# Preparing more chunks two ahead, and another order of the loads, in an attention and experts kernel

## The chip, the cores and the metric

The kernel runs on one core of one Trainium2 chip. The metric is the device time of one execution, in microseconds (us).

## The reference, cut to what matters

Three stages follow each other. A gated linear attention walks 768 tokens for each of 4 x 8 heads of width 48; its output, as 3072 tokens of 384 features, goes through a wide layer with a squared relu, and then through a soft mixture of 8 experts with 4 slots each.

```python
f = 1.0 / (1.0 + np.exp(-f_logit))
for t in range(S):                      # 768 steps, every head at once
    state = f[:, :, t, :, None] * state + np.einsum('bhd,bhe->bhde', k[:, :, t], v[:, :, t])
    y[:, :, t] = np.einsum('bhd,bhde->bhe', q[:, :, t], state)
x = y.transpose(0, 2, 1, 3).reshape(3072, 384)
h = np.maximum(x @ w_in, 0.0)           # 384 -> 2048
x = h * h @ w_out                       # 2048 -> 384
logits = x @ phi                        # 32 slots; softmax over tokens, and over slots
...                                     # slot inputs through the experts (384 -> 1024 -> 384), combined back
```

## The kernel before, in words

**Chunks.** The attention is worked in 24 chunks of 128 tokens (6 for each of the 4 sequences). For each chunk a load `fkq` (672 KB: gate logits, keys and queries, L136) and a load `v` (192 KB, L138) are issued by `chunk_load`. `fkq` lands in one of three places, chunk i in place i % 3, each with one buffer; `v` has three buffers. `prep(i)` turns them into running products of the gates (ACT L156, L158 or DVE L160, then four scans on DVE, L162), their inverses (ACT L169, L170), scaled keys (DVE L171) and scaled queries (DVE L177, L178, L179). The place of `fkq` is free again when the last of these, L179, has read it. `chunk(i)` is the rest: transposed keys (PE L193, ACT L195), scores (PE L205, DVE L208), states (PE L220, DVE L226 or L228), values (PE L243 and L250, ACT L254, DVE L259). Its six result DMAs (L265, L268) write the chunk into the token block `x`, on the SP queue, as every DMA of the kernel does.

**Blocks.** Four chunks make a block of 512 tokens, and there are 6 blocks. The wide layer goes over 16 slices of the hidden width, a step (b, ff) for each block and slice: layer 1 (three passes per product, L118 to L120, through `mm3`), relu and square on ACT (L369, L371, L372), the low part on DVE (L374), and layer 2 into three PSUM banks. The first four steps of block 0 run instead on whole fp32 weights (`layer1_whole`, L353, and L384). `TURNS` sets the order: block 0 with slices 0 to 3, block 1 with slices 0 to 8, then the remaining slices of both, then blocks 2 to 5 one by one.

**Weights.** Each slice's weights come as int64 patterns of a float64 (`w_load`, 768 KB, L305) and are split by ACT (L315, L319) and DVE (L320, L321, and L331 or L333), then into a high and a low part (L113, L114).

**What sets the order.** `stream()` writes out prep and chunk in pieces, five to a chunk (`STEPS`); `upto` draws as many pieces as a step's target wants. Before the first step of the wide layer, `FIRST` = 23 pieces are drawn, that is chunks 0 to 3 and three pieces of chunk 4. While i + 2 < `AHEAD` the chunk i carries prep(i + 2) with it, and from there on prep(i + 1). The text of the program is not its order on the engines: a scheduler takes the instructions by priority, which is the order in which they are written, and by when it reckons that their operands are ready; each engine, SP's queue too, then runs its own list strictly in that order and waits where a semaphore is not there yet. What `high_priority()` encloses is put ahead of what was written before.

**The loads.** Chunks 0 to 2 are loaded at the start, then two weight slices. Chunks 3 and 4 are loaded when chunks 0 and 1 are written to their end, each followed by one weight slice; from chunk 5 on chunk i + 2 is loaded in the second piece of chunk i. Further weight slices come at the head of a step (`while len(raw) < ...`), so that four are ahead of the one to be split.

Of the kernel before, what the change touches and what calls it, by code (L numbers as in the profile page):

```python
# [7 lines left out]
F32 = mybir.dt.float32  # L8
# [17 lines left out]
DM = H * D  # L26
NCH = B * S // C
# [8 lines left out]
SLOTS = 3  # L36
RAW = 5
WAHEAD = 4
AHEAD = 5
FIRST = 23  # L40
WARM = (3, 1, 3, 3)
OT = 1
# [15 lines left out]
class K:  # L58
# [70 lines left out]
    def chunk_load(self, i):  # L129
        nc, ap = self.nc, self.ap  # L130
        fkq = self.slot(i % SLOTS)[:DD].rearrange("d (x p t) -> d x p t", x=3, p=NP)
        if i == 0:
            nc.sync.dma_start(out=fkq[:, 0], in_=self.A["fkq"][i][:, 0])
            nc.sync.dma_start(out=fkq[:, 1:], in_=self.A["fkq"][i][:, 1:])
        else:
            nc.sync.dma_start(out=fkq, in_=self.A["fkq"][i])  # L136
        v = ap.tile([128, DM], F32, tag="v", name="v", bufs=3)
        nc.sync.dma_start(out=v, in_=self.A["v"][i])  # L138
        return fkq[:, 0], fkq[:, 1], fkq[:, 2], v

# [534 lines left out]
    def fast(self):  # L675
        with ExitStack() as main:
            self.fresh()
            self.wp = self.pool(main, "wp", bufs=NFF)
            fst = main.enter_context(ExitStack())
            self.fp = self.pool(fst, "fp")  # L680
            wst = fst.enter_context(ExitStack())
            self.wr = self.pool(wst, "wr")
            self.gp = self.pool(main, "gp", side="right")
            ast = main.enter_context(ExitStack())
            self.ap = self.pool(ast, "ap", side="right")
            self.attention_state(self.ap)
            self.loaded[0] = self.chunk_load(0)
            self.consts2()
            for i in (1, 2):
                self.loaded[i] = self.chunk_load(i)  # L690
            raw = {ff: self.w_load(ff) for ff in range(2)}
            pst = fst.enter_context(ExitStack())
            self.fast_blocks(main, pst, ast, wst, raw)
            self.tail()

    def fast_blocks(self, main, pst, ast, wst, raw):

        def stream():
            for i in range(2):
                yield from self.prep(i)  # L700
            for i in range(NCH):
                ahead = 2 if i + 2 < AHEAD else 1
                ch = self.chunk(i)
                pr = self.prep(i + ahead) if i + ahead < NCH and i + ahead not in self.U else iter(())
                for j, n in enumerate((1, 1, 0, 0, 2) if ahead == 2 else (1, 1, 1, 0, 2)):
                    next(ch)
                    for _ in range(n):
                        next(pr, None)
                    new = i + 3 if i < 2 else i + 2
                    if j == (4 if i < 2 else 1) and i != 2 and new < NCH:  # L710
                        self.loaded[new] = self.chunk_load(new)
                        if new < 5:
                            more_w()
                    yield

        def more_w():
            if len(raw) < NFF:
                raw[len(raw)] = self.w_load(len(raw))

        st = stream()  # L720
        for _ in range(8):
            next(st)
        done = 0
        end = NCH * STEPS

# [29 lines left out]
        def begin1(b, ff):  # L755
            if b == 0 and ff < WHOLE:
                return self.layer1_whole(b, ff)
            split(b)
            part(ff)
            return self.layer1(b, ff)  # L760
# [7 lines left out]
        self.w_split(0, raw[0], True)  # L768
        wn = 1
        posts = iter(())  # L770
        pend = begin1(0, 0)
        wait = 0
        for n, (b, ff) in enumerate(steps):
            if n == 3:
# [211 lines left out]
```

## Time and profile before

| | |
|---|---|
| runs | 601.58, 605.31, 607.11 us; median 605.31 |
| profiled execution | 606.27 us, its span 604.5 us |
| PE | 574.9 us busy, 5587 matmuls |
| DVE | 328.7 us busy |
| ACT | 314.8 us busy |
| DMA | 69.59 MB, mean 115 GB/s |

The span is what the profiler saw of one execution, and 1.8 us of its time lie around it. PE's busy time is modelled from pipelined matmuls: an engine that reads full may still run at half its clock, so a stretch is read with the granted clock beside it, and with how long equal groups of matmuls took. The profile's slices show DVE and ACT full up to about a quarter of the span and half idle behind it, while PE is full nearly all the way from there.

### The profile page before, as it was taken

What the parts mean: (1) busy time and instruction counts of PE and PEld (TensorE: products, weight loads), DVE (VectorE), ACT (ScalarE), POOL (GpSimd) and SP (SyncE); (2) the same over time, 40 slices, a digit from 0 to 9 for tenths busy, and PEclk for the clock granted to TensorE, in tenths of its full rate; (3) what the DMA queues carried; (4) which work ended last, traced back from release to release, by engine and by line L of the source; (5) the groups of instructions that cost most, each with busy time, mean ns of one, the idle gap of its engine ahead of it and who ended that gap; (6) DMA issues with size and microseconds to landing.
All of it is one profiled execution on the core that took longest, in us unless ns stands there. A gap on an engine that the chain in (4) does not pass through costs nothing.

```text
span 604.5 us, 13326 instructions
## 1 busy us (share of the span) xinstructions
PE 574.9 (95%) x5587; PEld 442.4 (73%) x5587; DVE 328.7 (54%) x688; ACT 314.8 (52%) x577; POOL 4.0 (1%) x10
## 2 busy tenths in 40 slices
PE   4899899999999999999999999999999999998993
PEld 3784467788787878778877777887788887886372
DVE  6978989999825547454464552543332322213322
ACT  5647759996635546354455354544334544442122
POOL 0000000000000000000000000000000100000000
PEclk9999979999999999999999999999999999999898
DMA  9557558421321202202211210220000745554757
GB/s 290 181 154 236 160 190 287 151 67 47 105 60 40 73 2 73 59 16 73 73 46 28 74 63 18 79 79 3 15 14 12 263 135 177 168 199 157 262 205 272
DMA packets 28324, 69.59 MB, mean 115 GB/s; under 512 B 4464, under 2 KB 17008, under 8 KB 28256
## 3 DMA queue, kind: packets, MB, share of 16 engines
q1 hardware_dynamic: 28256, 68.65, 35.8%
q8 instruction: 46, 0.75, 0.5%
q14 instruction: 22, 0.18, 0.1%
HBM read 59.20 MB, written 4.72 MB: 106 GB/s over the span
## 4 chain that ended last, share of the span: by engine, by line
PE 77%; DVE 7%; DMA 6%; ACT 6%; issue 2%; SPq 1%; ACTq 0%; DVEq 0%
PE o L118 10%; PE ph L118 9%; PE o L120 9%; PE ph L120 9%; PE ph L119 9%; PE o L119 9%; DMA g<-fkq 4%; PE psm L243 3%; DMA raw<-w 2%; DVE ip L162 2%; PE hp L591 2%; PE psm L220 2%; PE psm L205 2%; PE so L615 2%; PE o L384 1%
## 5 line engine op out<-in xcount | busy, mean ns | idle before, releaser
L374 DVE TENSOR_TENSOR gl<-r,gh 128x512 fp32r<-128x512 f32 x92 | 63.5, 690 | 119.2 <-ACT r L372 118.6
L369 ACT ACTIVATE r<-ph 128x512 f32<-128x512 f32 x92 | 54.7, 595 | 119.9 <-PE ph L120 114.9
L118 PE MATMUL o<-gh,w 128*128 128x512 f32 x276 | 112.8, 409 | 0.0
L118 PE MATMUL ph<-x,w 128*128 128x512 f32 x276 | 111.5, 404 | 0.0
L119 PE MATMUL o<-gh,w 128*128 128x512 f32 x276 | 108.0, 391 | 0.0
L120 PE MATMUL o<-gl,w 128*128 128x512 f32 x276 | 106.3, 395 | 1.8 <-DVE gl L374 1.7
L120 PE MATMUL ph<-x,w 128*128 128x512 f32 x276 | 107.8, 391 | 0.0
L119 PE MATMUL ph<-x,w 128*128 128x512 f32 x276 | 107.6, 390 | 0.0
L120 PEld LDWEIGHTS o<-gl,w 128*128 128x128 f32 x276 | 51.6, 188 | 15.7 <-DVE gl L374 4.8
L118 PEld LDWEIGHTS ph<-x,w 128*128 128x128 f32 x276 | 51.8, 188 | 14.7 <-issue 4.1
L118 PEld LDWEIGHTS o<-gh,w 128*128 128x128 f32 x276 | 51.7, 187 | 12.6 <-ACT gh L371 0.5
L120 PEld LDWEIGHTS ph<-x,w 128*128 128x128 f32 x276 | 51.8, 188 | 11.5
L371 ACT ACTIVATE gh<-r 128x512 fp32r<-128x512 f32 x92 | 58.3, 634 | 2.0
L119 PEld LDWEIGHTS ph<-x,w 128*128 128x128 f32 x276 | 51.9, 188 | 9.7
L372 ACT ACTIVATE r<-r 128x512 f32<-128x512 f32 x92 | 58.0, 630 | 1.8
L119 PEld LDWEIGHTS o<-gh,w 128*128 128x128 f32 x276 | 51.9, 188 | 9.4
L156 ACT ACTIVATE g<-g 112x512 f32<-112x512 f32 (+1 forms) x25 | 15.1, 609 | 41.8 <-DMA g<-fkq 41.8
L243 PEld LDWEIGHTS psm<-q,S 48*48 48x48 f32 (+1 forms) x704 | 27.2, 147 | 9.7 <-issue 4.6
L243 PE MATMUL psm<-q,S 48*48 48x64 f32 (+1 forms) x704 | 31.5, 244 | 2.5 <-DVE S L226 1.3
L162 DVE TENSOR_TENSOR_SCAN ip<-g,ip,big 112x128 f32<-112x128 f32 x80 | 33.4, 467 | 0.4 <-ACT g L158 0.2
L220 PEld LDWEIGHTS psm<-v,n 64*48 64x48 f32 (+1 forms) x704 | 21.3, 146 | 10.8 <-issue 5.3
L169 ACT ACTIVATE g<-ip 112x512 f32<-112x512 f32 (+1 forms) x25 | 15.3, 611 | 26.2 <-DVE ip L162 26.1
(143 smaller groups left out, 683.0 us busy)
## 6 DMA issues: line engine op xcount, KB each, us to landing
m<-m SPq DMA_DIRECT2D x26, 768.0 KB, 4.4
g<-fkq SPq DMA_DIRECT2D x23, 672.0 KB, 5.2
raw<-w SPq DMA_DIRECT2D x16, 768.0 KB, 7.1
v<-v SPq DMA_DIRECT2D x24, 192.0 KB, 3.6
g<-m SPq DMA_DIRECT2D x6, 768.0 KB, 4.5
out_dram<-ob SPq DMA_DIRECT2D x18, 256.0 KB, 3.3
x<-y SPq DMA_DIRECT2D x48, 72.0 KB, 2.8
x<-y SPq DMA_DIRECT2D x48, 16.0 KB, 1.8
```

Source lines behind the costliest of these rows:

```text
L118: mm(out=out, lhsT=sh, rhs=mh, start=start, stop=False)
L119: mm(out=out, lhsT=sl, rhs=mh, start=False, stop=False)
L120: mm(out=out, lhsT=sh, rhs=ml, start=False, stop=stop)
L156: nc.scalar.activation(f[:, s], f[:, s], AF.Exp, scale=-1.0)
L162: nc.vector.tensor_tensor_scan(ip[:, p], f[:, p], big, 1.0 if first else self.ip[:, p, C - 1 : C], ALU.mult, ALU.min)
L169: nc.scalar.activation(f[:, s], ip[:, s], AF.Ln)
L220: nc.tensor.matmul(out=pu[c][m, p], lhsT=U["n"][r, p, m], rhs=U["v"][r, hd * D : hd * D + D], start=True, stop=True)
L243: nc.tensor.matmul(out=pz[h * HR : h * HR + m, p, r], lhsT=U["S"][c][d, p * D : p * D + m], rhs=U["q"][d, p, r], start=True, stop=True)
L369: nc.scalar.activation(r, o, AF.Relu)
L371: nc.scalar.activation(gh, r, AF.Square)
L372: nc.scalar.activation(r, r, AF.Square)
L374: nc.vector.tensor_tensor(gl, r, gh.bitcast(F32), ALU.subtract)
```

## The change

`AHEAD` goes from 5 to 9, so that chunks 0 to 6, and not only 0 to 2, carry the preparation of the chunk two behind them; chunk 7 then carries none. The buffer of `v` gets a fourth place. The load of chunk 3 is issued right after the first two preparations are written, and the load of chunk i + 4 in the first piece of chunk i (in the fourth piece from chunk 8 on). The first two weight slices move behind the load of chunk 3, and within the stream a weight slice is asked for in a chunk's last piece, after its results, if fewer than four are ahead. The first step of the wide layer is written under `high_priority()`.

```diff
-AHEAD = 5
+AHEAD = 9
...
-        v = ap.tile([128, DM], F32, tag="v", name="v", bufs=3)
+        v = ap.tile([128, DM], F32, tag="v", name="v", bufs=4)
...
-            raw = {ff: self.w_load(ff) for ff in range(2)}
+            raw = {}
...
-                    new = i + 3 if i < 2 else i + 2
-                    if j == (4 if i < 2 else 1) and i != 2 and new < NCH:
+
+                    new = i + SLOTS + 1
+                    if j == (0 if i + 1 < AHEAD else 3) and new < NCH:
                         self.loaded[new] = self.chunk_load(new)
-                        if new < 5:
-                            more_w()
+                    if j == 4 and len(raw) < wn + WAHEAD:
+                        more_w()
                     yield
...
         st = stream()
+        wn = 0
         for _ in range(8):
             next(st)
+        self.loaded[SLOTS] = self.chunk_load(SLOTS)
+        for _ in range(2):
+            more_w()
...
-        pend = begin1(0, 0)
+        with self.tc.high_priority():
+            pend = begin1(0, 0)
```

## Rows read from the trace of the kernel before

**Rows 1.** Stretches: start:end, length; busy us (instructions) per engine; granted clock; DMA.
```profile
0.00:45.50 45.50, 33.65 (x644) 30.03 (x644) 35.01 (x82) 24.70 (x45) 1.10 (x8) 1.00 0.69 207
45.50:87.00 41.50, 38.21 (x435) 21.61 (x433) 36.41 (x72) 28.67 (x52) 0.00 (x0) 0.92 0.62 185
87.00:150.00 63.00, 62.82 (x485) 49.53 (x484) 62.32 (x104) 54.02 (x96) 0.00 (x0) 1.00 0.45 151
150.00:190.00 40.00, 38.42 (x282) 30.10 (x280) 21.18 (x45) 21.91 (x40) 0.00 (x0) 1.00 0.27 71
190.00:540.00 350.00, 349.36 (x3114) 277.88 (x3115) 154.43 (x331) 170.45 (x315) 2.85 (x2) 1.00 0.24 74
```

**Rows 2.** PE's timeline: start, length, line, form, count, idle before it.
```profile
43.03 1.48 PE L243 MATMUL psm<-q,S 48*64 48x64 f32 x23
45.55 4.13 PE L353 MATMUL ph<-x,wn 128*128 128x512 f32 x6
57.06 0.85 PE L243 MATMUL psm<-q,S 48*64 48x64 f32 x22 [0.19 <-DVE S L228]
78.57 1.48 PE L243 MATMUL psm<-q,S 48*64 48x64 f32 x23
```

**Rows 3.** PE's waits over the span: total us, times, longest.
```profile
PE psm L220 <- ACT n L195: 2.1, 1, 2.1
PE ph L353 <- DVE wn L331: 0.9, 1, 0.9
```

**Rows 4.** The chain of waits from 64 to 76 us: start, length, what.
```profile
64.78 7.78 DMA raw<-w
72.59 0.26 ACT raw L315
...
74.56 0.43 ACT n L195
75.04 0.75 PE psm L220 x14
```

**Rows 5.** Stretches of 3 us around the wait, and 30 to 45 us.
```profile
75.00:78.00 3.00, 2.96 (x24) 1.37 (x26) 1.97 (x5) 1.75 (x3) 0.00 (x0) 0.58 1.04 302
78.00:81.00 3.00, 3.00 (x80) 2.94 (x77) 2.14 (x4) 0.66 (x2) 0.00 (x0) 0.50 0.68 257
81.00:84.00 3.00, 3.00 (x9) 1.44 (x7) 2.51 (x5) 2.35 (x5) 0.00 (x0) 0.78 0.13 29
30.00:45.00 15.00, 14.22 (x308) 12.89 (x307) 11.13 (x24) 7.10 (x13) 0.00 (x0) 1.00 0.58 156
```

**Rows 6.** SP's timeline: start, length, line, what is loaded, count.
```profile
5.44 0.81 SPq L305 DMA_DIRECT2D raw<-w  x2
8.90 0.33 SPq L136 DMA_DIRECT2D g<-fkq  x1
...
36.57 0.58 SPq L136 DMA_DIRECT2D g<-fkq  x1
...
63.69 0.58 SPq L136 DMA_DIRECT2D g<-fkq  x1
```

**Rows 7.** DVE's timeline, pieces of one preparation.
```profile
45.95 1.61 DVE L162 TENSOR_TENSOR_SCAN ip<-g,ip,big 112x128 f32<-112x128 f32 x4
47.86 0.69 DVE L171 TENSOR_TENSOR k<-g,ip 112x512 f32<-112x512 f32 x1
```

**Rows 8.** ACT's timeline, with the idle time before a row in brackets.
```profile
18.56 0.91 ACT L315 ACTIVATE raw<-raw 128x768 int32<-128x768 uint32 x1
37.86 0.93 ACT L315 ACTIVATE raw<-raw 128x768 int32<-128x768 uint32 x1 [2.35 <-DMA raw<-w]
42.68 0.63 ACT L156 ACTIVATE g<-g 112x512 f32<-112x512 f32 x1 [1.78 <-DMA g<-fkq]
```

**Rows 9.** The weight loads, L305: issue to landing.
```profile
DMA to landing us min/median/max: 4.4/7.1/13.5
```

**Rows 10.** SP's waits over the span: total us, times, longest.
```profile
SPq L136 <- DVE q L179: 161.6, 13, 20.2
```

## The prediction

> **What bounds the kernel now.** First the table of stretches [rows 1]: from 87 to 150 us PE is busy 62.82 of 63 us, from 190 to 540 us 349.36 of 350, both at the full clock. There no wait is left to take away; the change neither adds nor removes a matmul, so whatever it gains must come from before 87 us, from the 1.6 us that PE idles between 150 and 190, or from nowhere. The first 87 us are the stretch to read closely, and they have two halves. Up to 45.5 us only attention runs (chunks 0 to 4), DVE is busy 35.0 us and PE 33.7. From 45.5 to 87 us chunks 5 to 7 run between the four whole-weight steps, with PE at 38.2 of 41.5 and a granted clock of 0.92.
>
> The second view is PE's timeline, for how long equal work takes [rows 2]: 23 matmuls of L243 take 1.48 us at 43 us and again at 78.6, while 22 of them take 0.85 at 57. At 78 to 81 us the granted clock is 0.50, the 1.2 GHz level [rows 5]. So the first 45 us run at that level too, though the clock column reads 1.00 there; the first six L353 at 45.55 still straddle the change. In this half PE is slow, but a chunk there is paced by the ring of ACT, PE and DVE around it, not by PE alone.
>
> The third view is the chain of waits behind the low clock [rows 4]. A weight slice (the seventh) was issued at 64.78, right behind a chunk's load at 63.69 [rows 6], and landed 7.78 us later. ACT stood in front of it at L315, and behind L315 in ACT's list stood the copy L195 that chunk 7's states wait for; PE waited 2.1 us [rows 3], and then ran at 0.58, 0.50 and 0.78 of its clock through three stretches [rows 5].
>
> **The change, part by part.**
>
> *Chunk loads earlier.* SP issued chunk 5's load at 36.57 [rows 6], behind result DMAs, and ACT then waited 1.78 us for it and began that preparation at 42.68 [rows 8]. With the load written in chunk 1's first piece it goes ahead of the results that held it. The same holds for chunks 4 and 6 to 8, one load each. The number of loads stays 24, so SP and the DMA engines carry no more; only the place changes. Past that the loads are as late as their place allows already: 13 of them wait on SP for L179, 161.6 us in all [rows 10]. There I take nothing, and for the 1.6 us of PE idle between 150 and 190 us [rows 1] also nothing, with bounds of 1.6 us to either side.
>
> *The stall at 72 us.* Chunk 8's load is no longer in front of the seventh weight slice, as it is asked for four chunks ahead. The fastest weight load took 4.4 us, this one 7.8 [rows 4, 9]; 3.4 us less is more than ACT's wait, so the 2.1 us on PE should go, and with them the low clock: 0.42, 0.50 and 0.22 of 3 us are 3.4 us of full-clock time [rows 5]. Term: -5.5 us; bounds 0 (another wait takes its place) and -5.5. I take the whole, as the profile names both parts in one chain.
>
> *Preparations moved forward.* One preparation costs DVE 1.61 us of scans and 0.69 for keys [rows 7] ahead of the same chunk's state and values, and three more of about that 0.69 behind them, 4.4 us with the keys. In 30 to 45 us DVE idled 15 - 11.13 = 3.9 us [rows 5], which is the room for the fifth chunk's. What does not fit there delays chunk 3, and so block 0 and the first L353 at 45.55 [rows 2]: at worst 1.61 + 0.69 = 2.3 us. Against it, those 4.4 us leave the second half, where DVE is at 36.4 of 41.5 and L353 once waited 0.9 us for a split weight [rows 3]. Net between +2.3 and -0.9; I take +0.7, the middle.
>
> *The first two weight slices behind chunk 3's load.* They were issued at 5.44 and would now go after 8.90 [rows 6], since SP waits there for chunk 0's place. ACT took the second at 18.56 without a wait [rows 8]. Issued near 10 us and at the median 7.1 us [rows 9], it lands near 17. So 0, with an upper bound: at the longest landing seen, 13.5 us, it is there at 23.5, and ACT would stand some 5 us. The fourth `v` place lets chunk 3's `v` go without waiting, and what is queued behind it are these same two loads.
>
> The skill has a rule against this part. By the Trainium skill (DMA: Bandwidth & Descriptors, Queues, rings and completion order) each DMA engine consumes one queue's descriptors in ring order, so a load that is put in front delays all that follow, however urgent. By it alone the weights could not overtake, and the sum would be that of the slower rival below; that the chunk load at 63.69 stood in front of the weights that landed 7.78 us later agrees with it.
>
> *Weights behind results, high priority.* The third and fourth slices keep their places; later ones come up to a step sooner. The first L353 already begins right behind chunk 4's values, when block 0's last results have landed, so the priority can only move ACT's relu and square ahead of a preparation: 0, between -0.6 and +0.6, one ACT operation of a preparation [rows 8].
>
> **Sum.** 606.27 - 5.5 + 0.7 = 601.5 us, against the profiled execution, which was 0.96 us above the median of 605.31. So 0.6% below the median. A difference under 1%, some 6 us, I count as no change, about what a measurement of this kernel can tell.
>
> **Rivals.**
>
> *A. Everything in the second half goes.* If DVE has prepared ahead and no ACT wait is left, PE's idle 3.3 us there (41.5 - 38.21) and the missing 0.08 of the clock over 41.5 us, another 3.3 [rows 1], go: 606.27 - 6.6 = 599.7, and with DVE's earlier idle time used for up to 3.9 us more [rows 5], 595.8. For it: DVE has the room. Against: work is in engine order and some wait always comes last. 596.
>
> *B. The wait is replaced.* The scheduler orders ACT's list by reckoned landings. Another load, still 4.4 to 13.5 us long [rows 9], stands in front of another copy; ACT waited 2.35 us for a weight slice at 37.86 as well [rows 8], which the change leaves where it is. Then the low clock comes back too: 605 to 608, 606.
>
> *C. Slower: the weights arrive late at the start.* Place: ACT's L315 at 18.56, in front of chunk 2's work. It decides if the second slice lands later than that; each us beyond is a us for all of chunks 2 and 3, to which the 2.3 us of DVE work may come, while the wait at 72 moves along and stays. Price up to 5 + 2.3: 608 to 613.5, near 611. For it: two more DMAs in front in the busiest stretch of the loads. Against: the median landing leaves 1.5 us of room.
>
> *D. It does little because the scheduler had done it already.* The 13 waits for L179 [rows 10] say that for later chunks it had; for chunk 5, issued at 36.57 behind results [rows 6], it had not. I put this into B.
>
> **How the numbers follow.** My forecast, 597.5 to 605, has 0.44; A (594 to 597.5) 0.18; B 0.20; C 0.18. One third of the forecast's stretch lies below 599.3, so faster by over 1% has 0.18 + 0.15 = 0.33; slower, above 611.4, is half of C with a little of B's tail, 0.11; the rest, 0.56, is within 1%. The range 595 to 609 leaves out about a third of A and two thirds of C, 0.18 in all. The forecast's own range is 597.5 to 605.
>
> The clock part can be weighed once more. By the Trainium skill (TensorE: Matmul & The Clock Gate, What's actually happening) the low level is the default and sustained activity releases it; the rows agree, the clock fell behind the 2.1 us wait and rose behind dense matmuls. By it alone a denser attention in the first 45 us would already run at the high level; PE reads 14.2 of 15 us busy there [rows 5] and takes 1.48 us for the group [rows 2], so I give that no gain.
>
> **What would show it.** Right: chunk 5's load on SP at least 5 us ahead of 36.57 and its first exp well before 42; no PE wait on L195 between 60 and 90 us, and the clock at 1.00 through it; the dense stretch that began at 87 us [rows 1] beginning 4 to 6 us sooner, and everything behind it moved by as much. Wrong: ACT idle in front of L315 before 24 us (C), a new stretch at 0.5 of the clock after 50 us (B), L353 starting after 46.5 us, or PE idle between 87 and 190 us that gives the lead back.

## The result and the profile after

The changed kernel takes 611.35 us (median of 4 runs, 610.21 to 613.95), the kernel before beside it on the same chip 604.55 (601.58 to 607.11). The ratio is 1.0119 with an interval of 1.0077 to 1.016: slower by about 1.2%, where 601.5 was forecast. The profiled execution is the slowest of the four, 613.95 us with a span of 612.2, against 606.27 and 604.5 before; 6.8 us lie between the medians, 7.7 between the spans.

The stretches after, with the columns of [rows 1]:

```profile
0.00:45.50 45.50, 30.42 (x591) 26.92 (x593) 38.24 (x92) 26.59 (x48) 1.10 (x8) 1.00 0.86 241
45.50:87.00 41.50, 39.22 (x467) 22.39 (x463) 35.94 (x73) 22.10 (x40) 0.00 (x0) 1.00 0.56 160
87.00:150.00 63.00, 60.43 (x415) 45.51 (x416) 58.23 (x91) 55.82 (x97) 0.00 (x0) 0.97 0.48 153
150.00:190.00 40.00, 39.14 (x343) 31.31 (x342) 20.56 (x45) 20.57 (x36) 0.00 (x0) 1.00 0.19 50
190.00:540.00 350.00, 347.92 (x3105) 275.57 (x3105) 154.85 (x331) 170.68 (x317) 2.85 (x2) 1.00 0.23 70
```

Three things stand out. Up to 45.5 us DVE did 3.2 us more than before and PE 3.2 us less. From 45.5 to 87 us PE is busier than before, and the clock column no longer falls (it reads 1.00 where the matmuls still run at the low level, as the second loss below shows). From 87 to 150 us, where PE had been full at the full clock, it now idles 2.6 us, at 0.97.

Busy time hides the clock, so I also count **lost time**: the length of a stretch less what its matmuls would take at the full clock without a pause. For this, each matmul is priced by its line from stretches at the full clock (L118 to L120 0.2267 us, L353 and L384 0.46, L193 0.11, L205 0.0195, L220 and L250 0.0225, L243 0.0315, others 0.11). By stretches, in us; it is good to about 2 us in the sum, as some records are missing:

| | to 45.5 | 45.5 to 65 | 65 to 87 | 87 to 95 | 95 to 190 | sum |
|---|---|---|---|---|---|---|
| before | 27.9 | 3.0 | 4.9 | 0.5 | 3.3 | 39.4 |
| after | 29.5 | 6.9 | 2.3 | 4.2 | 3.3 | 46.0 |

So 6.6 of the 7.7 us are lost before 95 us, in three places: +1.6 up to 45.5, +3.9 from 45.5 to 65, +3.7 from 87 to 95; and 2.6 are won from 65 to 87, where the forecast had put its gain.

**The first loss.** SP's timeline after, the first loads (chunks 3, 4 and 5, and the first two weight slices), to set beside [rows 6]; then ACT's timeline, beside [rows 8]; then the landings of the weights, beside [rows 9].

```profile
8.80 0.33 SPq L136 DMA_DIRECT2D g<-fkq  x1
...
9.64 0.91 SPq L305 DMA_DIRECT2D raw<-w  x2
16.67 0.33 SPq L136 DMA_DIRECT2D g<-fkq  x1
...
24.74 0.97 SPq L136 DMA_DIRECT2D g<-fkq  x1
```

```profile
19.17 0.91 ACT L315 ACTIVATE raw<-raw 128x768 int32<-128x768 uint32 x1 [0.46 <-DMA raw<-w]
...
22.28 0.91 ACT L315 ACTIVATE raw<-raw 128x768 int32<-128x768 uint32 x1 [1.32 <-DMA raw<-w]
```

```profile
DMA to landing us min/median/max: 4.2/6.2/12.2
```

The weights were issued at 9.64 us instead of 5.44, behind chunk 3's load; the second of them took the longest landing, 12.2 us, and ACT waited for both. Chunk 2's keys (L193) came at 25.65 us instead of 22.30. PE waits here too, up to 2.43 us for DVE's states (L228):

```profile
22.80 1.65 PE L243 MATMUL psm<-q,S 48*64 48x64 f32 x26 [2.43 <-DVE S L228]
```

The same wait stands at the same place in b2_weights_late (below), where only the start is changed and the weights are late. Chunk 5's load, on the other hand, is at 24.74 instead of 36.57, as the change means it.

**The second loss.** PE's timeline after, beside [rows 2] and, for a chunk's keys, beside the row of before that stands first here:

```profile
49.51 0.55 PE L193 MATMUL psm<-ident,k 112*128 112x112 f32 x4
```

```profile
45.21 1.48 PE L243 MATMUL psm<-q,S 48*64 48x64 f32 x23
...
48.13 1.01 PE L193 MATMUL psm<-ident,k 112*128 112x112 f32 x4 [0.33 <-ACT y L254]
...
52.78 2.07 PE L353 MATMUL ph<-x,wn 128*128 128x512 f32 x2
...
55.19 3.77 PE L353 MATMUL ph<-x,wn 128*128 128x512 f32 x4
58.89 0.73 PE L243 MATMUL psm<-q,S 48*64 48x64 f32 x18
```

The first L353 starts 7.2 us later than before, and between chunk 4's values and it now stand the keys, scores, states and half of the values of chunk 5, still at the slow pace (chunk 5's keys take 1.01 us instead of 0.55). From 45.5 to 65 us PE is busy 19.12 of 19.5 us, 18.39 before: what is lost here is pace, not idle time. The six L353 of the first step take 5.84 us in two groups, 4.13 before. DVE's timeline has changed as well. First before, then after, both from the states (L228) of chunk 4 on:

```profile
42.37 0.35 DVE L228 TENSOR_TENSOR S<-S,psm 112x192 f32<-112x192 f32 x1
43.32 0.35 DVE L228 TENSOR_TENSOR S<-S,psm 112x192 f32<-112x192 f32 x1 [0.60 <-PE psm L220]
45.58 0.42 DVE L259 TENSOR_TENSOR y<-y,psm 112x256 f32<-112x256 f32 x1 [1.91 <-PE psm L250]
45.95 1.61 DVE L162 TENSOR_TENSOR_SCAN ip<-g,ip,big 112x128 f32<-112x128 f32 x4
...
49.97 0.95 DVE L331 CUSTOM_DVE_ANT_0 wn<-raw,whi 128x1536 uint16<-128x1536 uint16 x1
```

```profile
44.56 0.34 DVE L228 TENSOR_TENSOR S<-S,psm 112x192 f32<-112x192 f32 x1
44.82 1.36 DVE L162 TENSOR_TENSOR_SCAN ip<-g,big 112x128 f32<-112x128 f32 x4
46.10 0.33 DVE L228 TENSOR_TENSOR S<-S,psm 112x192 f32<-112x192 f32 x1
...
55.61 0.95 DVE L331 CUSTOM_DVE_ANT_0 wn<-raw,whi 128x1536 uint16<-128x1536 uint16 x1
```

Before, DVE waited 0.60 us for the second state, and the scans of the next preparation came behind the chunk. After, the scans of a chunk that has been prepared early stand between two states, and the second weight split (L331) is 5.6 us later. Results stand in it too: in the chain of waits that ended last, a landing of chunk results comes before chunk 5's keys (ACT's copy of the values, L254, stands between the two). Before, that chain has no result DMA between 38 and 60 us.

```profile
43.28 4.22 DMA x<-y
48.13 1.01 PE psm L193 x4
```

PE's waits over the span, beside [rows 3], belong to the other two losses; the three for L228 lie at 22.80, 31.07 and 38.55 us:

```profile
PE psm L243 <- DVE S L228: 4.4, 3, 2.4
PE o L384 <- ACT g L357: 2.7, 1, 2.7
```

**The third loss.** The wait for L357 is the forecast's stall in another place. The slice is the seventh again, now issued at 79.33 us instead of 64.78, behind chunk 6's results. The chain after, beside [rows 4], then ACT's timeline, then stretches of 3 us, beside [rows 5]:

```profile
79.33 8.55 DMA raw<-w
87.90 0.88 ACT raw L315
89.35 3.65 PE o L384 x4
```

```profile
87.90 0.88 ACT L315 ACTIVATE raw<-raw 128x768 int32<-128x768 uint32 x1 [2.92 <-DMA raw<-w]
88.68 0.61 ACT L357 ACTIVATE g<-r 128x512 f32<-128x512 f32 x1
```

```profile
84.00:87.00 3.00, 2.70 (x9) 1.12 (x8) 2.81 (x6) 0.60 (x1) 0.00 (x0) 1.00 0.94 226
87.00:90.00 3.00, 0.65 (x1) 0.36 (x2) 0.76 (x1) 2.08 (x4) 0.00 (x0) 0.92 0.49 105
90.00:93.00 3.00, 3.00 (x5) 1.23 (x4) 1.68 (x3) 0.98 (x2) 0.00 (x0) 0.51 0.74 228
```

A weight slice again stands in front of ACT, with L357, for which PE waits, behind it; PE is busy 0.65 of 3 us, and then runs at 0.51 of its clock.

### The profile page after: what moved, and what is told of

Read it like the earlier page. It is cut to its first block, busy times and chain, and to the rows that moved or that the text cites. A ratio compares the mean times of both kernels' runs of the same rounds, so it can differ in the third digit from the quotient of the medians.

```text
span 612.2 us, 13316 instructions
## 1 busy us (share of the span) xinstructions
PE 577.2 (94%) x5587; PEld 442.3 (72%) x5587; DVE 329.0 (54%) x688; ACT 315.0 (51%) x577; POOL 4.0 (1%) x10
## 4 chain that ended last, share of the span: by engine, by line
PE 68%; DMA 10%; DVE 8%; ACT 8%; issue 2%; SPq 1%; ACTq 0%; DVEq 0%
PE o L118 9%; PE ph L118 9%; PE o L120 8%; PE ph L120 8%; PE ph L119 8%; PE o L119 8%; DMA g<-fkq 6%; DMA raw<-w 3%; PE psm L243 3%; DVE ip L162 3%; PE hp L591 2%; PE so L615 2%; PE psm L205 2%; ACT r L372 1%; PE psm L415 1%
## 5 line engine op out<-in xcount | busy, mean ns | idle before, releaser
L118 PE MATMUL o<-gh,w 128*128 128x512 f32 x276 | 112.7, 408 | 0.2 <-ACT gh L371 0.2
L118 PE MATMUL ph<-x,w 128*128 128x512 f32 x276 | 111.6, 404 | 0.2 <-ACT x L113 0.2
L120 PE MATMUL ph<-x,w 128*128 128x512 f32 x276 | 107.8, 391 | 0.0
L120 PE MATMUL o<-gl,w 128*128 128x512 f32 x276 | 106.1, 395 | 1.8 <-DVE gl L374 1.7
L118 PEld LDWEIGHTS ph<-x,w 128*128 128x128 f32 x276 | 51.8, 188 | 15.0 <-issue 4.1
L120 PEld LDWEIGHTS o<-gl,w 128*128 128x128 f32 x276 | 51.6, 188 | 15.3 <-DVE gl L374 4.3
L118 PEld LDWEIGHTS o<-gh,w 128*128 128x128 f32 x276 | 51.7, 187 | 12.6 <-ACT gh L371 0.3
L120 PEld LDWEIGHTS ph<-x,w 128*128 128x128 f32 x276 | 51.8, 188 | 11.8 <-DVE x L114 0.4
L243 PEld LDWEIGHTS psm<-q,S 48*48 48x48 f32 (+1 forms) x704 | 27.0, 144 | 17.2 <-issue 6.8
L243 PE MATMUL psm<-q,S 48*48 48x64 f32 (+1 forms) x704 | 32.0, 241 | 6.0 <-DVE S L228 4.4
L156 ACT ACTIVATE g<-g 112x512 f32<-112x512 f32 (+1 forms) x25 | 15.2, 610 | 42.1 <-DMA g<-fkq 42.1
L169 ACT ACTIVATE g<-ip 112x512 f32<-112x512 f32 (+1 forms) x25 | 15.3, 611 | 37.1 <-DVE ip L162 36.9
L162 DVE TENSOR_TENSOR_SCAN ip<-g,ip,big 112x128 f32<-112x128 f32 x80 | 33.1, 465 | 0.3
L220 PEld LDWEIGHTS psm<-v,n 64*48 64x48 f32 (+1 forms) x704 | 21.5, 146 | 9.6 <-issue 6.0
```

The costliest lines, as they stand in the source:

```text
L118: mm(out=out, lhsT=sh, rhs=mh, start=start, stop=False)
L120: mm(out=out, lhsT=sh, rhs=ml, start=False, stop=stop)
L156: nc.scalar.activation(f[:, s], f[:, s], AF.Exp, scale=-1.0)
L162: nc.vector.tensor_tensor_scan(ip[:, p], f[:, p], big, 1.0 if first else self.ip[:, p, C - 1 : C], ALU.mult, ALU.min)
L169: nc.scalar.activation(f[:, s], ip[:, s], AF.Ln)
L220: nc.tensor.matmul(out=pu[c][m, p], lhsT=U["n"][r, p, m], rhs=U["v"][r, hd * D : hd * D + D], start=True, stop=True)
```

## The experiments

Two theories stood at the start. **Theory 1**: one part of the change carries the loss, and taking it out gives it back. **The rival**: each wait that goes is replaced by the next one in some engine's list, so no part carries it. The table sums up all runs but the two with extra matmuls, which come at the end; each one stands beside the kernel before on the same chip. "PE waits" is the idle time of PE from 20 to 95 us that the profile puts down to a semaphore. The lost times are from the profiled execution, which may lie some us from the median.

| run | median us | ratio [interval] | PE waits | lost 45.5 to 65 | 65 to 87 | 87 to 95 |
|---|---|---|---|---|---|---|
| before | 604.3 to 604.9 | 1 | 5.1 | 3.0 | 4.9 | 0.5 |
| after | 611.35 | 1.0119 [1.0077, 1.016] | 10.0 | 6.9 | 2.3 | 4.2 |
| e1_weights_first | 608.91 | 1.0112 [1.007, 1.0154] | 7.2 | 6.3 | 1.8 | 0.3 |
| e2_ahead5 | 608.11 | 1.0059 [1.0034, 1.0085] | 10.4 | 6.8 | 1.6 | 1.5 |
| e1_e2_both | 607.46 | 1.006 [1.0035, 1.0085] | 11.1 | 4.0 | 1.9 | 1.2 |
| e4_weights_at_step | 610.68 | 1.0115 [1.0085, 1.0145] | 8.6 | 6.1 | 4.0 | 0.3 |
| e5_loads_behind | 610.9 | 1.0121 [1.0083, 1.016] | 8.8 | 5.1 | 4.0 | 3.9 |
| e6_step_first | 609.38 | 1.0062 [1.0042, 1.0082] | 13.8 | 6.8 | 3.0 | 0.6 |
| e7_split_first | 613.67 | 1.0148 [1.0117, 1.0179] | 13.2 | 3.2 | 2.5 | 2.2 |
| e1_e6_e7_together | 613.91 | 1.0149 [1.012, 1.0178] | 13.3 | 4.8 | 5.3 | 1.5 |
| b2_weights_late | 610.9 | 1.0085 [1.0062, 1.0109] | 9.3 | 2.3 | 6.0 | 2.0 |
| b3_load5_early | 610.75 | 1.0089 [1.0064, 1.0115] | 9.8 | 3.5 | 5.3 | 1.8 |
| b_loads_ahead | 607.34 | 1.0053 [1.0029, 1.0076] | 7.9 | 6.2 | 2.0 | 0.8 |
| b_weights_behind | 607.5 | 1.0049 [1.0025, 1.0074] | 8.0 | 3.0 | 5.8 | 1.7 |
| b4_wahead5 | 607.87 | 1.0056 [1.0037, 1.0076] | 7.8 | 2.7 | 2.5 | 4.1 |
| b_split_first | 609.41 | 1.008 [1.0052, 1.0108] | 11.8 | 5.3 | 3.4 | 0.2 |
| b_split_wahead5 | 613.84 | 1.0151 [1.0117, 1.0185] | 14.9 | 4.1 | 3.8 | 1.4 |
| b_v4 | 604.66 | 0.9993 [0.9974, 1.0013] | 5.7 | 2.0 | 3.6 | -0.2 |

### Taking parts out of the changed kernel

**e1_weights_first.**

```diff
-            raw = {}
+            raw = {ff: self.w_load(ff) for ff in range(2)}
...
-        for _ in range(2):
-            more_w()
```

> The changed kernel with the first two weight slices loaded ahead of everything again, as before the change. In the changed kernel the two slices were issued at 10 us and ACT waited 0.46 and 1.32 us for them (L315 at 19.2 and 22.3), with chunk 2's L169 behind the second; chunk 2's first matmul came 3.35 us later than before. Late first weights (my rival C): both waits vanish, chunk 2's L193 comes near 22.3 instead of 25.65, the first L353 some 3 us sooner, time down by 3 us or more (near 608). Preparation and loads pushed ahead: DVE's queue is what delays chunk 2, PE's 4.4 us of waits for L228 stay, and the time falls by less than 1 us (610 to 612).

ACT's waits at L315 before 24 us are gone, chunk 2's keys come at 22.09, and the stall at 87 us has gone too; but chunks 3 and 4 are only 0.9 and 0.4 us sooner, since PE now waits 2.73 us for states (L228) at 30.21. What it gives back is uncertain: by the ratio, 1.0112, next to nothing, by the medians 0.4% (608.91 is 0.70% above the kernel before); one of the six runs took 615.18. The late weights are real, and another wait takes part of their place.

**e2_ahead5.**

```diff
-AHEAD = 9
+AHEAD = 5
```

> The changed kernel with AHEAD = 5 again, so only the number of chunks prepared two ahead goes back; the loads stay early (from chunk 4 on in the fourth piece). Preparation ahead as the cause: chunk 5's matmuls and preparation no longer stand in front of the first L353, which comes near 46 to 48 us instead of 52.8, PE's waits for L228 shrink below 2 us, and the time falls by 4 to 7 us (604 to 607). Loads or weights as the cause: first L353 stays past 51 us and the time within 2 us of the changed kernel.

About half of the loss returns. The first L353 still starts at 52.84, so the second loss does not hang on `AHEAD`; what the table has less is from 65 to 95 us, above all from 87 (1.5 lost instead of 4.2).

**e4_weights_at_step, e5_loads_behind.** The weight slices back at the head of a step, and the chunk loads behind a chunk's results:

```diff
-                    if j == 4 and len(raw) < wn + WAHEAD:
+                    if j == 4 and i < 2:
```

```diff
-                    if j == (0 if i + 1 < AHEAD else 3) and new < NCH:
+                    if j == 4 and new < NCH:
```

> The changed kernel with the weight slices after the fourth asked for at the head of a step again (only chunks 0 and 1 bring one in their last piece). In the changed kernel the seventh slice was issued at 79.3 us behind chunk 6's results, landed 8.55 us later, ACT stood 2.9 us in front of it, PE 2.7 us, and the clock fell to 0.51 at 90 to 93 us. Weights behind results as a cause: that stall goes and with it 4 to 5 us (near 606.5). Only the first half as the cause: the dense stretch starts as late as in the changed kernel, another wait takes the place, and the time stays within 2 us.

> The changed kernel with each chunk load written in the last piece of a chunk, behind its results, instead of in the first, two ahead as in the change. Loads ahead of results as the cause: the 72 KB result DMAs land in 2.8 us again (4.0 in the changed kernel), preparations start later and the scans no longer stand in front of L228 on DVE, the first L353 comes by 48 us and the time falls by 3 to 6 us. Late first weights as the cause: ACT's waits at L315 near 19 and 22 us stay, and so does the time within 2 us.

Neither gives anything back. With e5 the results land in 2.3 us (median, 2.8 before) and chunk 5's load goes out at 31.48 us, yet the first L353 starts at 50.48, not by 48, and 5.1 us are lost from 45.5 to 65. With e4 the stall at 87 us goes (0.3 lost instead of 4.2), and 2.6 us of that appear again from 65 to 87 us (4.0) and from 95 to 190 (4.2 instead of 3.3).

**e6_step_first.** Chunk 5's keys and scores are held on PE until the first whole-weight product is done.

```diff
+        with self.tc.issue_after(self.gate) if i == 5 else ExitStack():
-        self.knat(i)
-        self.scores(i)
+            self.knat(i)
+            self.scores(i)
```

> The changed kernel, but chunk 5's transposes and scores are queued on PE behind the six matmuls of the first whole-weight step, as they stood before the change (in the changed kernel chunk 5's preparation is done early and its matmuls stand in front of that step, which then starts at 52.8 us). The order as the cause, with chunk 5 worked at the low clock: the six start near 49 us, when block 0's last results have landed, the full clock comes some 3 us sooner, the stretch of 45 to 65 us gives back 2.5 to 4 us and the time falls to 607 to 608.5. The order as a mere consequence (the step waits for block 0's results or its weights either way): six matmuls still past 51.5 us and the time within 1.5 us of the changed kernel.

The first L353 starts at 47.27, as expected, and nothing of the 6.8 us from 45.5 to 65 returns: PE stood 4.5 us before the second group of the step (the lines are one further here):

```profile
47.27 3.17 PE L354 MATMUL ph<-x,wn 128*128 128x512 f32 x6
54.97 4.43 PE L354 MATMUL ph<-x,wn 128*128 128x512 f32 x6 [4.53 <-DVE wn L332]
```

So the order on PE is not the cause in itself; the late second split on DVE was next in line. The time does fall, to 1.0062, about half of the loss; but by the table that comes from 87 to 95 us (0.6 lost instead of 4.2), which the edit was not meant for.

**e7_split_first.**

```diff
-        self.w_split(0, raw[0], True)
+        with self.tc.high_priority():
+            self.w_split(0, raw[0], True)
...
-                self.w_split(wn, raw[wn], wn < WHOLE)
+                with self.tc.high_priority() if wn < WHOLE else ExitStack():
+                    self.w_split(wn, raw[wn], wn < WHOLE)
```

> The changed kernel, with the splits of the first four weight slices (ACT L315 and L319, DVE L320 to L333) written under high priority, so that they stand on ACT and DVE ahead of the preparations written before them; nothing else. Theory 1 (the common cause between 45 and 65 us is DVE: the scans of chunks prepared two ahead stand in front of the split of the second slice, whose last part starts at 55.61 instead of 49.97 us): the second L331 starts by 51 us, the 5 us between the first and the second group of the whole-weight step are gone, and 2 to 4 us of the 7 lost there return: 607 to 609.5 us. Rival (the replaced wait: moving the split ahead only moves the scans behind it, so chunks 2 to 4 come later by as much, and ACT waits at L315 for data that has not landed): L353 begins later than 53 us, the loss up to 45 us grows from 29.5 to over 31 us, and the time is 610.5 to 614.

Both lose a part. The second L331 did not come sooner (56.18), the first L353 starts at 53.22, and up to 45.5 us 30.7 are lost, short of the rival's 31; the stretch from 45.5 to 65 improves to 3.2 in the profiled execution, which at 609.94 was the fastest of six. But the median of 613.67 is the rival's: PE's wait for the states is now a single one of 5.7 us, as the splits stand in front of them.

**e1_e6_e7_together.** The three edits above at once.

> The changed kernel with three things at once: the first two weight slices loaded ahead of chunk 3 again, chunk 5's scores held back on PE until the first whole-weight product is done, and the splits of the first four slices under high priority. Theory 1 (the causes are separate and add up: late first weights, the order on PE, the split late on DVE, each hidden behind the next when one alone is taken away): the losses of 45 to 65 and of 87 to 95 us both go, 603 to 606 us, as fast as the kernel before. Rival (each wait removed is replaced by the next in the queue of another engine): no better than the best single one, 607.5 to 610 us.

613.91: worse than e1 and e6 alone, and no better than e7. The separate causes do not add up.

**e1_e2_both.** The edits of e1 and e2 at once.

> The changed kernel with the first two weight slices loaded ahead of chunk 3 again, and with AHEAD at 5 again; the early chunk loads, the weights behind results and v in four places stay. If the two parts carry the loss together (they gave back 2.4 and 3.2 us singly): 604 to 606.5 us, and the first L353 starts before 48 us. If the early loads alone are enough for it, as the run with only chunk 5's load earlier (610.75) suggests: 608 to 611 us, with an ACT wait at L315 or a stretch at half the clock between 60 and 95 us.

607.46, no better than e2 alone. What is left of the change in it, at 0.6%, is the early loads, the weights behind results, the places of `v` and the high priority of the first step.

### Putting parts into the kernel before

**b2_weights_late, b3_load5_early, b4_wahead5.** The first two slices behind chunk 3's load (`v` in four places); chunk 5's load alone moved, to chunk 2's first piece (`v` in four places here too); and, to test the forecast's main term, a fifth slice ahead.

```diff
-            raw = {ff: self.w_load(ff) for ff in range(2)}
+            raw = {}
...
-                        self.loaded[new] = self.chunk_load(new)
+                        if new != SLOTS:
+                            self.loaded[new] = self.chunk_load(new)
...
+        self.loaded[SLOTS] = self.chunk_load(SLOTS)
+        for _ in range(2):
+            more_w()
```

```diff
-                    new = i + 3 if i < 2 else i + 2
-                    if j == (4 if i < 2 else 1) and i != 2 and new < NCH:
+                    new = i + 3 if i < 3 else i + 2
+                    if j == (4 if i < 2 else 0 if i == 2 else 1) and i != 3 and new < NCH:
```

```diff
-WAHEAD = 4
+WAHEAD = 5
```

> The kernel before, with only the start changed: chunk 3's load, and then the first two weight slices, are issued after the first two preparations (and v has four places); everything else as before. Late first weights (my rival C): ACT waits 1 to 2 us at the second slice near 22 us, chunk 2 starts 3 us later, the first step 1 to 3 us later, and the kernel is 1 to 3 us slower than before. If the wait is absorbed by chunk 3 and 4, as the removal of this part from the changed kernel suggests (0.9 us at block 0's results), the time is within 1.5 us of before.

> The kernel before, with only chunk 5's load issued earlier (written at the head of chunk 2 and so ahead of chunk 2's results; v has four places). My prediction took such an earlier load as free or a gain: time 603 to 605. Loads and preparation ahead as the cause of the loss: chunk 5's scans stand in front of chunk 3's and 4's states on DVE, chunk 5 or the results of chunk 2 and 3 come later, the first step starts 1 to 3 us later and the time is 1 to 3 us above before.

> The kernel before, with weight slices asked for five ahead instead of four, so that the seventh is issued a step earlier and nothing else moves on purpose. My term for the stall at 72 us: ACT's wait at that slice and PE's 2.1 us behind it go, the clock stays at 1.00 from 50 us on, and the kernel is 3 to 5.5 us faster than before (599 to 601.5). The stall is replaced by another one in the queues: no change, within 1.5 us.

b2 and b3 each cost nearly as much as the whole change, +0.85 and +0.89%. Both keep the stall that the forecast wanted gone, 2.6 and 4.4 us later in time: the ACT wait at L315 is 1.70 at 75.18 us and 1.85 at 76.94, and the clock reads 0.50 behind it. Their first L353 starts at 46.25 and 46.36, and neither has the second loss (2.3 and 3.5 us). b4 removes that stall, and the clock column stays at 1.00 from 48 to 84 us; then it gets another one. PE's timeline, ACT's and a stretch of 4 us:

```profile
85.72 0.50 PE L118 MATMUL ph<-x,w 128*128 128x512 f32 x1 [0.65 <-ACT x L113]
```

```profile
87.99 1.14 ACT L113 CAST x<-x 128x512 fp32r<-128x512 f32 x2 [2.32 <-DMA x<-y]
```

```profile
88.00:92.00 4.00, 3.67 (x9) 2.62 (x9) 3.36 (x5) 1.50 (x3) 0.00 (x0) 0.50 0.99 324
```

This one is of another make than the third loss after: ACT stands in front of the next block's tokens, whose results have not landed, and not in front of a weight slice. With one constant changed, the low clock comes back near 88 us behind a new wait, and 4.1 us are lost from 87 to 95. (A wait of 2.0 us for L357 is in b4 as well, at 51.09 us.)

**b_loads_ahead, b_weights_behind.** The early chunk loads, and the weights behind results. The first of the two is not the loads alone: `v` has four places in it, and the first step's high priority stands in it as in the changed kernel, though its expectation names the loads alone.

```diff
-                    new = i + 3 if i < 2 else i + 2
-                    if j == (4 if i < 2 else 1) and i != 2 and new < NCH:
+                    new = i + SLOTS + 1
+                    if j == (0 if i + 1 < AHEAD else 3) and new < NCH:
...
+        self.loaded[SLOTS] = self.chunk_load(SLOTS)
...
-        pend = begin1(0, 0)
+        with self.tc.high_priority():
+            pend = begin1(0, 0)
```

```diff
-                        if new < 5:
-                            more_w()
+                    if j == 4 and len(raw) < wn + WAHEAD:
+                        more_w()
```

> The kernel before with the chunk loads alone asked for four chunks ahead (v in four places; weights, preparations as before). If the loads carry what is left: 607.5 to 611 us, results' DMAs landing near 4 us instead of 2.8, the weight slices 2 to 4 later than before, and the first L353 after 48 us. If they are harmless once the weights stand first: 603 to 606 us, with chunk 5's load before 32 us and its preparation sooner.

> The kernel before, where a weight slice is asked for in a chunk's last piece, behind its results, if fewer than four are ahead; chunk loads, preparations and the first two slices as before. If this part is harmless (a slice comes up to a step sooner, and nothing behind the loads changes): 603 to 606 us, the seventh slice ahead of or behind chunk 8's load, the stall at 72 us in its place or shorter. If it carries what is left of the loss: 607 to 610 us, with a weight slice in front of a chunk's load on SP and ACT waiting for that chunk at L156.

b_loads_ahead, with `AHEAD` at 5 and the weights first, has a second loss of the same size: the first L353 at 52.89 (after: 52.78), 6.2 us lost from 45.5 to 65 (after: 6.9). Part of it is idle time here: PE is busy 16.66 of these 19.5 us (after: 19.12). The weights were not late, slices 3 and 4 at 23.31 and 31.22 us against 23.21 and 30.69. The results landed in 3.4 us instead of 2.8, and ACT's copy L254 at 38.99 waited 3.14 us, by the profile for such a landing; so the queue is not ruled out. DVE's timeline of b_loads_ahead, then PE's:

```profile
43.74 0.35 DVE L228 TENSOR_TENSOR S<-S,psm 112x192 f32<-112x192 f32 x1
...
44.61 1.36 DVE L162 TENSOR_TENSOR_SCAN ip<-g,big 112x128 f32<-112x128 f32 x4
...
47.81 0.69 DVE L177 TENSOR_TENSOR t<-ip,g 112x512 f32<-112x512 f32 x1
48.41 0.75 DVE L259 TENSOR_TENSOR y<-y,psm 112x256 f32<-112x256 f32 x2
```

```profile
47.90 0.60 PE L193 MATMUL psm<-ident,k 112*128 112x112 f32 x4 [1.93 <-ACT y L254]
```

and its stretches of 3 us:

```profile
45.00:48.00 3.00, 1.07 (x34) 0.92 (x28) 3.00 (x8) 1.75 (x3) 0.00 (x0) 1.00 0.61 139
48.00:51.00 3.00, 2.44 (x54) 2.07 (x56) 2.96 (x7) 2.20 (x4) 0.00 (x0) 0.70 0.85 277
51.00:54.00 3.00, 3.00 (x30) 2.31 (x31) 2.96 (x8) 0.93 (x3) 0.00 (x0) 0.50 1.00 239
```

The scans (L162) of a preparation stand ahead of the values (L259) of chunk 4, which were at 45.58 and 47.48 before and come at 48.41. ACT's copy L254, for which PE waits 1.93 us, comes at 47.27 instead of 44.80: in ACT's list it stands behind L169, which waited 1.88 us for those scans. From 45 to 48 us DVE is full, and PE is busy 1.07 us of 3.

A rival stays untested here: the high priority. The runs without it that leave the splits in place (b2, b3, b4, b_weights_behind, b_v4, b_warm_start) start the first L353 at 45.15 to 47.71 us; every run with it, e6 apart, where chunk 5's matmuls are held back, at 50.48 to 54.03. All the runs with it have the chunk loads moved as well, so the two can't be told apart: no run takes the line out of the changed kernel or puts it alone into the kernel before. That such a line can move the start by so much shows b_split_first below (51.07), where it stands around the splits. b3, without it, has one load early and +0.89%, but no second loss.

b_weights_behind has no second loss (3.0), and not the wait for a chunk's load at L156 that was expected, but a stall at 72 us that has grown. ACT waits up to 3.2 us at L315 and PE 3.1 us for L195, and the stretches read:

```profile
72.00:75.00 3.00, 1.13 (x37) 0.85 (x35) 3.00 (x7) 0.61 (x1) 0.00 (x0) 1.00 0.91 180
75.00:78.00 3.00, 1.76 (x17) 1.33 (x18) 0.82 (x3) 3.00 (x7) 0.00 (x0) 0.73 0.60 125
```

**b_split_first, b_split_wahead5.** The edit of e7 in the kernel before, without and with `WAHEAD = 5`.

> The kernel before, with the splits of the first four weight slices under high priority, and nothing else. If DVE's place for the split is what limits the stretch from 45 to 65 us, there is little to take here, as only 3.0 us are lost in it: 603.5 to 605 us. If the order of DVE and ACT is a balance in which what is moved forward delays the chunks behind it: 605.5 to 609 us, with the first L353 after 46 us.

> The kernel before with the same splits first, and five weight slices asked for ahead instead of four (which alone, at 607.87, took away the stall at 72 us and got another one at 88). If the new stall comes from the late splits of the whole-weight slices, both stalls go: 600 to 603 us, the 5.5 us that were forecast. If a wait is always replaced: 605 to 609 us, with a stretch at half the clock somewhere between 65 and 95 us.

Both fall on the side of the balance, above the ranges given for it, and the second, meant to collect the forecast's 5.5 us, is 1.5% slower: PE waits 5.7 us for states, in two waits (in e7 in one).

### The control and the clock

**b_v4.**

```diff
-        v = ap.tile([128, DM], F32, tag="v", name="v", bufs=3)
+        v = ap.tile([128, DM], F32, tag="v", name="v", bufs=4)
```

> The kernel before with v in four places and nothing else; every engine's list is the same, on SP alone one load of v moves up and splits a run of weight loads. If the order of before is so finely balanced that any move costs: 606.5 to 610 us. If not, as no engine's order changes: 603.5 to 606 us, the stall at 72 us in its place.

604.66, ratio 0.9993. With the same lists on PE, DVE and ACT the time is the same, though a load on SP moved. Of the eighteen kernels that ran with another order (after included, and the two below, which have more matmuls), every one is slower, by 0.5 to 1.6%.

**b_warm_start, a_warm.** Matmuls that nobody reads, ahead of the attention, and in a_warm also in the gaps of chunks 0 to 2:

```diff
+            self.warm(20, self.sums[3])
             self.loaded[0] = self.chunk_load(0)
...
         self.knat(i)
+        if i < 3:
+            self.warm(4, self.ident)
...
         self.state(i)
+        if i < 2:
+            self.warm(4, self.ident)
```

> The kernel before with 20 matmuls of 128 x 128 zeros (one of the state tiles, cleared at the start) on PE ahead of the attention, whose results nobody reads; the scheduler's order behind them shifts a little. If steady work lifts the clock and the attention keeps it up: 23 matmuls of L243 take 0.85 us instead of 1.48 from chunk 1 on, chunks 1 to 4 come up to 1.5 us each sooner, and the time is 598 to 603 us. If the attention's matmuls with their gaps do not hold the clock: L243 stays at 1.48 us and the time is 604 to 609 us, the difference being the order alone.

> The changed kernel with the same 20 matmuls at the start and four more of 128 x 128 in each of the gaps of chunks 0 to 2 (behind the transposed keys, and behind the states of chunks 0 and 1). If the low clock of the first 55 us carries the loss: L243 at 0.85 us, the loss from 45 to 65 us falls from 6.9 to about 4 and the time to 603 to 607 us. If the waits carry it and the clock only follows them: L243 at 1.48 us still, or faster without effect, and 609 to 614 us.

610.66 us, ratio 1.0088 [1.0059, 1.0116], and 614.14, ratio 1.0156 [1.0126, 1.0185]. The clock did rise: four L193 take 0.55 us at 8.86 us in b_warm_start, instead of 1.01, and 0.60 at 16.26 in a_warm. It fell again, at about 16 us and 24. Of a_warm:

```profile
16.00:20.00 4.00, 3.50 (x78) 2.98 (x67) 4.00 (x10) 3.52 (x8) 0.00 (x0) 1.00 0.96 361
20.00:24.00 4.00, 1.71 (x33) 1.33 (x33) 4.00 (x10) 2.99 (x5) 0.00 (x0) 1.00 1.04 223
24.00:28.00 4.00, 3.75 (x78) 3.10 (x76) 3.90 (x8) 3.42 (x8) 0.00 (x0) 0.56 0.54 172
```

The useless matmuls held chunk 0's keys up to 9.26 us in a_warm (after: 6.39). By chunk 2 the faster PE had made up 2.4 of these 2.9 us (26.12, after: 25.65), and later nothing (chunk 5's keys at 48.95, after: 48.13); DVE was full by then, 4.00 of 4 us. In b_warm_start chunk 1 came 1.0 us sooner than before, at 13.86, and chunk 2 1.1 us later, at 23.42. So the low clock at the start is worth some 2 us here, which DVE takes over and the matmuls cost. Whether it costs by itself from 45 to 55 us stays open, as the clock had fallen by then.

## Why the prediction was wrong, point by point

**The stall at 72 us, -5.5: the step that failed.** "I take the whole, as the profile names both parts in one chain." Both parts went: 65 to 87 us is at the full clock, and 2.6 us were won there. But the step took it that the slice would land faster ("3.4 us less is more than ACT's wait"), and the part on the weights that later slices "come up to a step sooner". The seventh was issued 14.6 us later, at 79.33, and took 8.55 us to land, not 4.4, behind a chunk's results. ACT's list kept a weight slice in front of something that PE needs, and the wait came back at 87 us, with the low clock: +3.7. The other bound of this very term, 0 ("another wait takes its place"), was rival B, and got too small a chance. b4_wahead5 shows with one constant that another wait takes its place, with the low clock, though there it is for results and not for a weight slice; and b_weights_behind shows that the part of the change meant for the weights makes the stall longer. Between the forecast and the profiled execution lie 12.5 us: 6.6 are this term's (1.1 lost instead of 5.5 won), 4.8 come from the first two losses (5.5, where the sum had 0.7), and the rest lies behind 190 us.

**Chunk loads earlier, 0.** "There I take nothing" counted only who waits for the loads. That the load also decides where the scheduler places the preparation on DVE was left out, though the text said that the order goes by when operands are reckoned ready. One load moved, in b3, costs 0.89%; all of them, with the high priority, 0.53% in b_loads_ahead, some 3 us, with a second loss. What the loads do without the high priority was not measured beyond b3.

**Preparations moved forward, +0.7.** The bound of 2.3 us was for one preparation in front of chunk 3. In the changed kernel DVE does 3.2 us more before 45.5 us, which is more than the bound; but with `AHEAD` at 5 again (e2) it does 3.7 us more, and 6.8 us are lost from 45.5 to 65. So neither hangs on this part: DVE's work moves forward in the runs with early loads, whatever `AHEAD` is (b_loads_ahead 3.5 us more, e1_e2_both 4.6). `AHEAD` alone is worth about half a per cent: 1.0119 against 1.0059, with intervals that just overlap (e2 also puts the loads from chunk 4 on into the fourth piece). That is some 3.6 us where the sum had 0.7; in e2's table row 2.7 of it are from 87 to 95 us.

**The first two weight slices, 0, with an upper bound of 5.** The bound was nearer than the value: the second landed after 12.2 us where I had taken the median of 7.1, and chunk 2 was 3.35 us late. The median was the wrong row, since it is taken over all sixteen weight loads, and this one stood behind chunk 3's load and the first slice. The Trainium skill's rule, cited in the prediction (DMA: Bandwidth & Descriptors, Queues, rings and completion order), that a queue's descriptors are consumed in order, agrees with this number. b2_weights_late puts the part at +0.85%; e1_weights_first gives back between 0.07% (ratios) and 0.4% (medians).

**Weights behind results, high priority, 0.** For the weights +0.49% [0.25, 0.74] alone. The high priority was never run by itself, so its bounds of 0.6 us stand untested. `v` in four places, 0, was right (b_v4).

**The rivals.** C's number, near 611, was met, and its sign was there, ACT idle before L315 ahead of 24 us. That its size fits is luck: the price was 5 us of waiting and 2.3 of DVE's work, and up to 45.5 us only 1.6 were lost; without the late weights 0.7 to 1.1% remain (e1). B had the mechanism that the third loss and b4 show, a replaced wait, at too small a price, as it had no loss ahead of 65 us in it. Of the signs, the early load came (chunk 5's at 24.74), and so did all four of being wrong: ACT idle at L315, 0.51 of the clock at 90 us, L353 at 52.78 and PE idle behind 87 us. One slip in the chances changes nothing: 1.8 of the forecast's 7.5 us lie below 599.3, a quarter and not a third.

**What is shown and what is not.** Shown: where the 6.6 us are lost; that the second is PE's work at the low level for longer, with a later first L353; that the third is a replaced wait; that the late first weights and the weights behind results cost 0.85 and 0.49% alone, and the early loads with the high priority 0.53%, 1.9% if they added, against 1.2% for the whole change with `AHEAD` besides. Not shown: whether the second loss is due to the early loads, to the high priority of the first step or to both; and whether the results' later landings have a share in it. Nor is a single cause shown. What the runs allow is that the order of before, with 5.1 us of PE waits from 20 to 95 us, is a balance; every other order that was run has 7.2 to 14.9. But the waits don't rank the runs: e1_e2_both has 11.1 at 607.46, after 10.0 at 611.35. No version beat the kernel before.

## What to carry to other kernels

Before a load is moved earlier in a program that a scheduler orders, ask what work becomes ready with it, and on which engine's list that work then stands in front of something urgent: here it was DVE, and ACT behind it; whether the queue paid too stayed open. A stall that is named in one chain is worth at most what the next-latest arrival allows; take the whole only where the list behind it holds no second wait of the same kind. And put each part alone into the old kernel, not only take it out of the new one: here taking out one part hid what others did. Then hold the whole edit against the old kernel: the high priority, left in b_loads_ahead, keeps its result from being that of the loads.

## What the runs showed of the hardware

- The granted clock reads 1.00 from the start until the first change that the trace records. That the first 45 us run at the 1.2 GHz level shows in durations (L243 x23 in 1.48 us) and, once a run has raised the clock early, in the column: 0.50 from 20 to 48 us in b_warm_start, with the same 1.48.
- In a_warm the clock fell behind a stretch of 4 us in which PE was busy 1.71 us, in b_warm_start behind one of 1.91; behind 3.50 of 4 it had stayed. Twice the speed of PE there made up 2.4 us over two chunks, and nothing behind them.
- A weight slice of 768 KB took 4.4 to 13.5 us to land before and 4.2 to 12.2 after; the longest after stood behind chunk 3's load and another slice. The median landing of the results' 72 KB went from 2.8 to 4.0 us with the loads in front, and to 2.3 with the loads behind (e5).
